# Input x by transposing DMAs in natural row order instead of TensorE transposes, in a fused spectral and state-space kernel

## The chip, the cores and the metric

The kernel runs on one core of a Trainium2 chip. The metric is the device time of one execution in microseconds (us). Five engines run side by side, each with its own queue of instructions that it takes in order: TensorE (PE: matmuls, and the transposes that are written as matmuls), VectorE (DVE), ScalarE (ACT), GpSimd (POOL) and SyncE (SP, which here only issues DMAs). An instruction starts when its engine is free and the data and buffers that it needs are ready.

## The reference

The input x has 2048 tokens of 1024 channels in bf16. Two branches are computed and mixed token by token with a gate:

```python
g = sigmoid((x * gate_w).sum(-1, keepdims=True))
# A: filter in the frequency domain
a = irfft2(rfft2(x) * (w_r + 1j * w_i)).astype(bfloat16)
# B: complex diagonal recurrence with 1024 states
Lam_bar = exp(exp(log_dt) * Lambda)
Bu = x @ (((Lam_bar - 1) / Lambda)[:, None] * Bmat).T
h[t] = Lam_bar * h[t - 1] + Bu[t]
b = 2 * real(h @ Cmat.T) + x * Dskip
out = g * a + (1 - g) * b
```

## The kernel before

**x in two roles.** The tile `xQ` holds x transposed: channels on partitions, in 8 blocks `d8`, and for each of 16 rows j the 128 tokens m*16+j. It is made by `load_x` (L195, eight plain loads of 512 KB into the space of the tiles `CT`, which C fills later) and `turn_x` (L653): eight TensorE transposes into a PSUM tile `pt`, and a copy by ScalarE to `xQ` (L657). That copy also puts the even and the odd m of a row into two halves.

**The front.** `front()` (L768) works through the 16 rows of the spectral branch. Of a row, `fold(j)` (L659) adds and subtracts the two halves of the channels on VectorE into `preT`; `fd(j)` (L332) is the transform along the channels, eight matmuls with the constant `G`, copied out as `X1` (L339); `s1(j)` (L342) is the first step of the transform along the tokens, four matmuls with the constant `T2`, copied out as `A1` (L351) and stored to a scratch in DRAM by SyncE (L353). Before row 8 VectorE does the copy of `A1`, from row 8 on ScalarE. `keep_A1` keeps one column in every 512 of `A1`.

**The tables.** The recurrence is done as a rotation, a real scan, and a rotation back. The rotations need four tables of cosines and sines, made by `make_tab` (L208) for two of eight blocks of states at a time. It is cut into pieces by `yield`, and `front(n)` takes n pieces behind each row. In order, the pieces hold: VectorE's angle and its reduction (L213, L814, L816); ScalarE's Abs and Sin (L818, L819); ScalarE's cosine and scaled sine (L821, L224), with a copy by GpSimd; ScalarE's scaled cosine (L229) with VectorE's first product (L230); VectorE's second product (L235), which shares a piece with the next block's angle. A block of 45 lines of small operations (L825 to L855) runs on VectorE before the tables; it waits for ScalarE's first sines and cosines, and the fold of row 5 is queued behind it.

**The recurrence.** `unit(c, q)` (L253) handles 256 tokens and half of the states, in two halves of 32 matmuls from `xQ` and B into PSUM `psu` (L300), each copied out by ScalarE as `h` (L302). All 16 rows of x enter each of them. Its VectorE work is put into a list `work` as seven pieces with their due costs, 12.7 in all (turn back 2.4, join 1.5, two scans of 2.3, carry 0.4, turn 2.4, join on 1.4), and `vector(us)` takes pieces from that list up to the given amount. `early(tb)` (L579) is the product with C for 128 tokens, also in two halves. `halves(ssm, n)` advances a chain of units and early tiles by n halves. The units 0,0 / 0,1 / 1,0 / 1,1 make up the first eight halves.

**The order by hand.** PE, VectorE and ScalarE run in program order (`manual_schedule`, L169). From row 8 on, each row of the front is followed by one half of the chain, from row 9 with `vector(4.2)`; the matmuls of the gate (L695) stand behind row 10. After the front come seven stages of gfnet, "w", "a", "z", "q", "qn", "s2" and "uv", which correct single columns and start the next transform, with 4, 1, 2, 2, 1, 0 and 1 halves between them and `vector(3.0)` after each half; "w" begins with small matmuls that reverse a vector (L390). Then 16 steps "is1" (L484, L485) follow with one half each, 16 steps "is2", and the output tiles.

**The queues.** SyncE issues the loads of x, G, T2, B, the small constants and C, and the stores of `A1`; B and C are loaded by transposing DMAs (L205, L555). GpSimd issues ten small DMAs of columns of W (`load_Wcols`, L733, behind row 3) and two DMAs of the gate. The order on these two queues is chosen by a scheduler.

**PSUM.** `psA` has two buffers, shared by `fd`, `s1` and the small products; the transposes have two (`psX`), the units one (`psF`) until row 7 and then two (`psU`).

Of the kernel before, what the change touches and what calls it, by code (L numbers as in the profile page):

```python
# [13 lines left out]
FP32 = mybir.dt.float32  # L14
# [14 lines left out]
NHA, NHB = 4, 2  # L29

# [78 lines left out]
def kernel(  # L109
# [55 lines left out]
    xctx = ExitStack()  # L165
    psF = xctx.enter_context(tc.tile_pool(name="psF", bufs=1, space=PSUM, reuse_waits="tile"))
    psX = xctx.enter_context(tc.tile_pool(name="psX", bufs=2, space=PSUM, reuse_waits="tile"))
    pools = {"u": psF}
# [3 lines left out]

    vec8 = tmp.tile([8, 5, P], BF16, name="vec8")
# [13 lines left out]
    xn = [CT[i // 4][:, 2 * (i % 4):2 * (i % 4) + 2, :] for i in range(8)]  # L187
    x_v = x.rearrange("(p j) d -> p j d", j=16)
    fft = {}
    fft["G"] = pre.tile([P, 2, 4, K], BF16, name="G_sb")  # L190
# [3 lines left out]
    def load_x(i):  # L194
        nc.sync.dma_start(out=xn[i], in_=x_v[:, 2 * i:2 * i + 2, :])  # L195
# [55 lines left out]
    x_t = xQ.rearrange("p d j (g q) -> p d g j q", g=2)  # L251

    def unit(c, q):  # L253
# [42 lines left out]
        for ri in range(2):  # L296
            psu = pools["u"].tile([P, 4, TC], FP32, name="psu", tag="psu")
            for j in range(4):
                for d8 in range(8):
                    nc.tensor.matmul(psu[:, j, :], lhsT=BT[4 * q + j][:, ri, d8, :],  # L300
                                     rhs=x_t[:, d8, :, :, 8 * c:8 * (c + 1)], start=(d8 == 0), stop=(d8 == 7))
            nc.scalar.copy(out=u[:, ri].rearrange("p b (q j) -> p b q j", j=32),  # L302
                           in_=psu.rearrange("p b (j q) -> p b q j", j=32))
# [23 lines left out]
    def gfnet():  # L327
# [4 lines left out]
        def fd(j):  # L332
            ps = psA.tile([P, 2, K], FP32, name="ps_fd", tag="ps")
# [5 lines left out]
            (nc.vector.tensor_copy if j in (3,5,7,) else nc.scalar.copy)(out=X1.rearrange("p r (i c) -> p r i c", c=2), in_=ps.rearrange("p c (r i) -> p r i c", r=2))  # L339
            X1s[j] = X1  # L340

        def s1(j):  # L342
# [7 lines left out]
            A1 = CT[0][:, j, :].rearrange("p (g k) -> p g k", g=2) if j < 8 else A1_4[:, j % 4]  # L350
            (nc.vector.tensor_copy if j < 8 else nc.scalar.copy)(out=A1, in_=psa)  # L351
            A1s[j] = A1
            nc.sync.dma_start(out=t1_w[j], in_=A1)  # L353
            if j in (8, 12):
                keep_A1(j - 4)

        def keep_A1(j):
            if j < 8:
# [322 lines left out]
    for i in range(3, 8):  # L681
        load_x(i)
# [287 lines left out]
```

## Time and profile before

| | |
|---|---|
| time, median of 3 runs | 340.88 us (340.6 to 340.92) |
| span of the profiled execution | 338.3 us, from its first to its last instruction |
| busy share of PE, DVE, ACT, POOL | 96%, 86%, 49%, 10% |
| granted TensorE clock | full throughout |
| 128 transposes (L656), busy 0.61 us for eight | within the first 34 us |
| plain loads of x (L195) | 8 of 512 KB, 5.8 us to landing |
| first half of the recurrence, start | 40.46 us |
| first VectorE work of the recurrence, start | 51.81 us |
| last `s1` of the front, start | 81.57 us |
| first "is1" matmul, start | 129.06 us |

The profiled execution's own time is known as its span; the timed runs of the same kernel are 2.6 us above it in the median, which is the work before the first and after the last instruction. Times inside the execution are counted from the start of the span. A matmul is listed with its whole passage through the array, so the next one starts before the listed end: 32 matmuls of a half take 3.67 us, and the next instruction starts 3.5 us after the first.

### The profile page before, as it was taken

What the parts mean: (1) busy time and instruction counts of PE and PEld (TensorE: products, weight loads), DVE (VectorE), ACT (ScalarE), POOL (GpSimd) and SP (SyncE); (2) the same over time, 40 slices, a digit from 0 to 9 for tenths busy, and PEclk for the clock granted to TensorE, in tenths of its full rate; (3) what the DMA queues carried; (4) which work ended last, traced back from release to release, by engine and by line L of the source; (5) the groups of instructions that cost most, each with busy time, mean ns of one, the idle gap of its engine ahead of it and who ended that gap; (6) DMA issues with size and microseconds to landing.
All of it is one profiled execution on the core that took longest, in us unless ns stands there. A gap on an engine that the chain in (4) does not pass through costs nothing.

```text
span 338.3 us, 6201 instructions
## 1 busy us (share of the span) xinstructions
PE 326.3 (96%) x2414; PEld 212.3 (63%) x2446; DVE 292.1 (86%) x449; ACT 167.0 (49%) x211; POOL 32.1 (10%) x64
## 2 busy tenths in 40 slices
PE   8989899999999999999999999999999999999995
PEld 3445465666847575747566575869945876565552
DVE  2679948999999999999999999999980997999951
ACT  3697597836223145656557552646632243443510
POOL 1372012210000000000000000000000011121220
PEclk9999999999999999999999999999999999999999
DMA  7999999998893047889999735947203019856695
GB/s 263 409 192 212 203 217 213 163 215 205 274 213 102 2 129 180 227 202 272 259 284 260 200 135 153 224 127 215 62 2 125 32 31 147 168 109 94 110 145 166
DMA packets 83581, 58.71 MB, mean 174 GB/s; under 512 B 54328, under 2 KB 74304, under 8 KB 83424
## 3 DMA queue, kind: packets, MB, share of 16 engines
q1 hardware_dynamic: 80304, 55.64, 65.5%
q0 software_dynamic: 3168, 2.66, 8.3%
q8 instruction: 19, 0.31, 0.4%
q14 instruction: 10, 0.08, 0.1%
q10 hardware_dynamic: 80, 0.01, 0.0%
HBM read 30.49 MB, written 17.83 MB: 143 GB/s over the span
## 4 chain that ended last, share of the span: by engine, by line
PE 71%; DVE 23%; ACT 2%; issue 2%; DVEq 0%; ACTq 0%
PE ps_y L570 26%; PE psu L300 22%; PE ps_h L570 4%; DVE h L275 4%; PE ps_id L601 4%; PE ps_is L484 2%; PE ps_fd L336 2%; PE ps_is L509 2%; PE ps_is L485 2%; DVE CT L351 2%; PE ps_y L574 2%; PE ps_s L460 2%; DVE h L263 1%; DVE su L262 1%; DVE h L287 1%
## 5 line engine op out<-in xcount | busy, mean ns | idle before, releaser
L300 PE MATMUL psu<-xQ,BT 128*128 128x256 bf16 x1024 | 116.6, 273 | 0.8 <-ACT ye L588 0.5
L300 PEld LDWEIGHTS <-BT 128*128 128x128 bf16 x1024 | 98.8, 98 | 17.5 <-issue 4.5
L570 PE MATMUL ps_y<-CT,h 128*128 128x512 bf16 x436 | 99.5, 379 | 0.6
L570 PEld LDWEIGHTS <-h 128*128 128x128 bf16 x512 | 49.7, 98 | 55.2
L275 DVE TENSOR_TENSOR_SCAN h<-rz,h 128x1024 bf16<-128x1024 f32 x32 | 72.2, 2280 | 0.3
L302 ACT CAST h<-psu 128x1024 bf16<-128x1024 f32 x32 | 32.3, 1011 | 51.4 <-PE psu L300 51.3
L616 POOL DMA_DIRECT2D BT<-y_scratch x10 | 11.9, 1194 | 239.6 <-DVE BT L610 232.0
L588 ACT ACTIVATE ye<-ps_y,omg 128x512 f32<-128x512 f32 x20 | 12.7, 684 | 44.0 <-PE ps_y L574 28.7
L336 PE MATMUL ps_fd<-G_sb,preT 128*128 128x512 bf16 x119 | 29.3, 379 | 2.1 <-ACT X L339 1.0
L262 DVE TENSOR_TENSOR su<-h,tab 128x2048 bf16<-128x2048 bf16 x16 | 19.6, 1223 | 2.8 <-ACT h L302 2.2
L336 PEld LDWEIGHTS <-preT 128*128 128x128 bf16 x128 | 12.0, 97 | 15.4 <-issue 2.8
L287 DVE TENSOR_TENSOR h<-h,tab 128x2048 bf16<-128x2048 bf16 x16 | 20.7, 1295 | 0.5
L462 ACT CAST X<-ps_s 128x1024 bf16<-128x1024 f32 x16 | 16.2, 1014 | 8.7 <-PE ps_s L460 8.7
L263 DVE TENSOR_TENSOR h<-h,tab 128x2048 bf16<-128x2048 bf16 x16 | 19.6, 1225 | 0.8
L286 DVE TENSOR_TENSOR sg<-h,tab 128x2048 bf16<-128x2048 bf16 x16 | 19.5, 1220 | 0.1
L657 ACT COPY xQ<-pt 128x1024 bf16<-128x1024 bf16 x16 | 15.6, 1017 | 2.8 <-PE pt L656 2.7
L511 ACT CAST ZT<-ps_is 128x1024 bf16<-128x1024 f32 x16 | 15.5, 1024 | 2.2 <-PE ps_is L509 2.2
L339 ACT CAST X<-ps_fd 128x1024 bf16<-128x1024 f32 x13 | 13.2, 1012 | 6.2 <-PE ps_fd L336 6.1
L487 ACT CAST C<-ps_is 128x1024 bf16<-128x1024 f32 x16 | 16.1, 1007 | 0.0
L601 PE MATMUL ps_id<-raw,ZT 128*128 128x256 bf16 x128 | 15.9, 273 | 0.0
L570 PE MATMUL ps_h<-CT,h 128*128 128x512 bf16 x62 | 14.4, 379 | 0.1
L601 PEld LDWEIGHTS <-ZT 128*128 128x128 bf16 x128 | 12.4, 98 | 2.2
(186 smaller groups left out, 362.3 us busy)
## 6 DMA issues: line engine op xcount, KB each, us to landing
y_scratch<-ye SPq DMA_DIRECT2D x20, 256.0 KB, 2.6
CT<-in_A_x_dram SPq DMA_DIRECT2D x8, 512.0 KB, 5.8
Bb<-turn_scratch SPq DMA_DIRECT2D x16, 256.0 KB, 4.0
turn_scratch<-C SPq DMA_DIRECT2D x16, 256.0 KB, 3.7
raw<-turn_scratch SPq DMA_DIRECT2D x16, 256.0 KB, 4.2
Wb<-in_A_w_r_dram SPq DMA_DIRECT2D x32, 127.8 KB, 4.2
Wb<-in_A_w_i_dram SPq DMA_DIRECT2D x32, 127.8 KB, 4.1
out_dram<-BT SPq DMA_DIRECT2D x14, 256.0 KB, 2.5
```

What stands on the lines that cost most here:

```text
L262: nc.vector.tensor_mul(out=su, in0=u[:, ::-1], in1=bc(1))
L263: nc.vector.tensor_mul(out=u, in0=u, in1=bc(0))
L275: nc.vector.tensor_tensor_scan(out=seg, data0=rz[:, js].rearrange("p j t -> p (j t)"), data1=seg, initial=0.0, op0=ALU.mult, op1=ALU.add)
L286: nc.vector.tensor_mul(out=sg, in0=u[:, ::-1], in1=bc(3))
L287: nc.vector.tensor_mul(out=u, in0=u, in1=bc(2))
L300: nc.tensor.matmul(psu[:, j, :], lhsT=BT[4 * q + j][:, ri, d8, :], rhs=x_t[:, d8, :, :, 8 * c:8 * (c + 1)], start=(d8 == 0), stop=(d8 == 7))
L302: nc.scalar.copy(out=u[:, ri].rearrange("p b (q j) -> p b q j", j=32), in_=psu.rearrange("p b (j q) -> p b q j", j=32))
L336: nc.tensor.matmul(ps[:, cls, :], lhsT=preTs[j][:, 4 * cls + d4, :], rhs=G_sb[:, cls, d4, :], start=(d4 == 0), stop=(d4 == 3))
L462: nc.scalar.copy(out=X2, in_=ps2)
L487: nc.scalar.copy(out=C1.rearrange("p h (c i) -> p h c i", c=2), in_=psc.rearrange("p h (i c) -> p h c i", c=2))
L570: nc.tensor.matmul(psy, lhsT=hs[c, jb // 4][:, ri, jb % 4, P * tq:P * (tq + 1)], rhs=CT[ri][:, jb, 512 * dh:512 * (dh + 1)], start=(i == 0 ...
L601: nc.tensor.matmul(pse[:, slot, :], lhsT=ZT_t[:, i, tb, :], rhs=fft["Gi"][:, i, :], start=(kb == 0), stop=(kb == 1))
```

## The change

- x is loaded by 16 transposing DMAs on SyncE, one for each row j, straight into `xQ`, with the tokens of a row in natural order. `turn_x`, its copies, and one group of four `keep_warm` matmuls are gone.
- The split into even and odd m moves into `fold`, which now reads `xQ` with a step of two elements. The units and the gate read `xQ` in natural order, and their copies out of PSUM are adapted.
- The order on SyncE is written anew: x and the first eight loads of B interleaved, T2 in between, then the small constants, the other eight of B, and all of C behind the front. G is issued by ScalarE, ahead of the five small vectors.
- Of the `A1` copies, VectorE does rows 6, 8, 10, 12, 14 and 15 and ScalarE the other ten. All sixteen go to `CT` and are stored by GpSimd. ScalarE does all the copies of `X1` (before, VectorE did three).
- `fd` uses the two buffers of `psU`, which the units now have from the start; `psA` is left to `s1` and the small products.
- `front` is the same for all rows: fold two rows ahead, `fd` one row ahead, `s1`, then the table pieces: none to row 3, one for rows 4 to 7, two from row 8. The recurrence joins in from row 14, with one half and `vector(2.0)` behind each of rows 14 and 15. The gate, `keep_A1(1)` and the remaining loads follow the front, then six halves with `vector(3.5)` each, and the stages "w" to "uv" get 7, 1, 1, 1, 1, 0 and 1 halves. `load_Wcols` moves from row 3 to row 12. The chain has unit 2,1 before the first early tile.

```diff
+A1_BY_VECTOR = (6, 8, 10, 12, 14, 15)
...
+    for cls in range(2):
+        nc.scalar.dma_start(out=fft["G"][:, cls], in_=cG[:, cls])
...
-    x_v = x.rearrange("(p j) d -> p j d", j=16)
+    x_v = x.rearrange("(m j) d -> j m d", j=16)
...
-    def load_x(i):
-        nc.sync.dma_start(out=xn[i], in_=x_v[:, 2 * i:2 * i + 2, :])
+    def load_x(j):
+        nc.sync.dma_start_transpose(out=xQ[:, :, j, :], in_=x_v[j])
...
-            ps = psA.tile([P, 2, K], FP32, name="ps_fd", tag="ps")
+            ps = psU.tile([P, 2, K], FP32, name="ps_fd", tag="psu")
...
-            A1 = CT[0][:, j, :].rearrange("p (g k) -> p g k", g=2) if j < 8 else A1_4[:, j % 4]
-            (nc.vector.tensor_copy if j < 8 else nc.scalar.copy)(out=A1, in_=psa)
-            A1s[j] = A1
-            nc.sync.dma_start(out=t1_w[j], in_=A1)
+            A1 = CT[j // 8][:, j % 8, :].rearrange("p (g k) -> p g k", g=2)
+            (nc.vector.tensor_copy if j in A1_BY_VECTOR else nc.scalar.copy)(out=A1, in_=psa)
+            nc.gpsimd.dma_start(out=t1_w[j], in_=A1)
...
-        nc.vector.tensor_add(out=preTs[j][:, 0:4], in0=xQ[:, 0:4, j, :], in1=xQ[:, 4:8, j, :])
-        nc.vector.tensor_sub(out=preTs[j][:, 4:8], in0=xQ[:, 0:4, j, :], in1=xQ[:, 4:8, j, :])
+        to = preTs[j].rearrange("p d (g q) -> p d g q", g=2)
+        lo, hi = (xQ[:, 4 * i:4 * (i + 1), j, :].rearrange("p d (q g) -> p d g q", g=2) for i in range(2))
+        nc.vector.tensor_add(out=to[:, 0:4], in0=lo, in1=hi)
+        nc.vector.tensor_sub(out=to[:, 4:8], in0=lo, in1=hi)
...
+    for j, b in enumerate((0, 0, 0, 0, 0, 1, 0, 1, 0, 1, 0, 1, 1, 1, 1, 1)):
+        load_x(j)
+        if j in (1, 2, 6):
+            load_T2(*{1: (0, 2), 2: (2, 8), 6: (8, 16)}[j])
+        load_B(b)
     assert step() == "front"
-    for j in range(2):
-        turn_x(j)
-        fold(j)
-    keep_warm(4)
+    fold(0)
     fft["fd"](0)
+    fold(1)
...
-        for what in plan.get(j, "fFS"):
...
+        if j + 2 < 16:
+            fold(j + 2)
+        if j + 1 < 16:
+            fft["fd"](j + 1)
+        fft["s1"](j)
...
-        front(0 if j < 4 else 1 if j < 6 else 2 if j < 10 else 3)
-        if j >= 8:
+        front(0 if j < 4 else 1 if j < 8 else 2)
+        if j == 8:
+            fft["keep_A1"](0)
+        if j == 12:
+            load_Wcols()
+        if j >= 14:
             halves(ssm, 1)
-        if j >= 9:
-            vector(4.2)
...
+            vector(2.0)
+    gate()
+    fft["keep_A1"](1)
+    load_small()
+    load_B(8)
...
+    for q in range(8):
         load_C(q)
-    for v, n in (("w", 4), ("a", 1), ("z", 2), ("q", 2), ("qn", 1), ("s2", 0), ("uv", 1)):
+    for _ in range(6):
+        halves(ssm, 1)
+        vector(3.5)
+    for v, n in (("w", 7), ("a", 1), ("z", 1), ("q", 1), ("qn", 1), ("s2", 0), ("uv", 1)):
```

## The prediction

> **What bounds the kernel now.** I read the page first. Its share by engine says that TensorE is nearly full and VectorE not far behind:
>
> ```profile
> span 338.3 us, 6201 instructions
> PE 326.3 (96%) x2414; PEld 212.3 (63%) x2446; DVE 292.1 (86%) x449; ACT 167.0 (49%) x211; POOL 32.1 (10%) x64
> ```
>
> The reader is to see that 12 us of TensorE's span are idle, and that a change is worth what it does to TensorE's queue, or to VectorE's where TensorE waits for it. Next the busy time by stretch, cut at the last row before the recurrence, at the end of the eighth half (85.6), at the first "is1" (129.06) and at the end of that phase; behind the length come PE, PEld, DVE, ACT and POOL:
>
> ```profile
> 7.15:39.92 32.77, 29.34 (x225) 15.22 (x230) 27.84 (x73) 24.81 (x34) 12.83 (x33) 1.00 1.11 265
> 39.92:85.60 45.68, 44.92 (x364) 30.82 (x369) 39.41 (x61) 31.38 (x44) 6.38 (x14) 1.00 1.04 203
> 85.60:129.20 43.60, 42.57 (x350) 29.77 (x352) 41.45 (x75) 13.38 (x17) 0.00 (x0) 1.00 0.56 140
> 129.20:206.60 77.40, 76.98 (x503) 48.45 (x509) 75.84 (x91) 43.58 (x60) 0.00 (x0) 1.00 0.82 221
> ```
>
> From 39.92 on TensorE is full, because each row of the front is followed by a half of the recurrence. From 85.6 VectorE is full too. Last the chain of waits around row 8 (start, us, what), one turn of a loop between VectorE and ScalarE:
>
> ```profile
> 38.99 0.79 DVE tab L235 x2
> 39.77 0.54 DVE ang L213 x2
> ...
> 40.34 0.44 DVE rot_kk L814
> ...
> 40.80 0.70 DVE ang L816
> ...
> 42.58 0.99 ACT X L339
> 43.57 0.91 ACT A L351
> 44.49 0.62 ACT cs_f L821
> 45.11 0.40 ACT t L224
> 45.53 0.92 DVE tab L230 x2
> ...
> 47.12 0.79 DVE tab L235 x2
> ```
>
> From L235 to the next L235 it takes 8.13 us for two rows. VectorE's angle must be done before ScalarE's Abs and Sin; these stand before the copies of `X1` and `A1`, these before the cosine, and VectorE's next product waits for that, with the next fold queued behind it. In the kernel before TensorE has halves of 3.5 us to do meanwhile. That cover is what the change takes away.
>
> **The change part by part.** Prices from the chain and the timeline: eight transposes 0.45 us of TensorE's queue (16 in 0.89), an `fd` 1.74, an `s1` 0.54, a half 3.5 (32 matmuls in 3.49), the gate 1.83 (55.79 to 57.63).
>
> *Transposes, copies, keep_warm.* Before `s1(8)`, 14 groups of transposes go, 6.3 us of TensorE; 16 copies of ScalarE of 1.02 and four `keep_warm` matmuls (1.03, in a gap) go too. ScalarE gets three more `X1` and two more `A1` of 1.01. The second buffer of `psU` for `fd` lets it run one row ahead, so there I let TensorE go at its own pace, 2.28 a row.
>
> *Rows 0 to 8.* The first `fd` stays at 7.15: G landed 6.0 us after an issue at 1.19, and ScalarE issues it only half a microsecond earlier. `s1(8)` has ten `fd`, eight `s1` and a 0.2 us transpose of the vectors ahead: 21.9 us. In between stands the block of small operations, 3.2 us long (21.91 to 25.1). ScalarE's `X1(2)` starts at 13.3 (7.15, three `fd`, one `s1`, 0.2, 0.2 of passage); behind it come `A1(1)`, Abs 0.2, a table load 1.28, Sin 0.2, `X1(3)` and `A1(2)`: with copies at 0.91 each the cosine runs at 18.6, the block at 18.9 to 22.1, and `fd(5)` at 22.9, where TensorE was free at 18.4. So `s1(8)` starts at 7.15 + 21.9 + 4.5 + 0.2 = 33.8, against 39.92: 6.1 us gained here.
>
> *Rows 8 to 14.* The turn of 8.13 stays, as the pieces come at two per row. It gets longer by `A1` of the even row, now on VectorE between the fold and L235 (1.14), and by the fold's step of two. No row has a bf16 operation with such a step; the ends are 0.42 (the contiguous L661, same size) and 0.69 (L816, the same size in f32), so 0 or 0.54 per turn. I take the upper end: what is read lies 4 bytes apart, as in the f32 row. Turn: 8.13 + 1.14 + 0.54 = 9.8.
>
> [...]
>
> The first L235 comes at 33.8 + 0.65 + 1.15 = 35.6 (behind `A1(8)`), the next at 45.4 and 55.2. Behind the third are the angle and its reduction (2.4), so `fold(15)` runs at 57.6, `fd(15)` at 58.3, `s1(14)` at 60.0. TensorE needed 6 x 2.28 = 13.7 of these 26 us. The two halves behind rows 14 and 15 end at 60.6 + 3.5 + 0.54 + 3.5 = 68.1; gate and six halves: 90.9. The eighth half, gate included, ended at 85.6 before. TensorE is 5.3 late.
>
> *The recurrence on VectorE.* Its first piece needs the second half's copy: 68.1 + 1.2 = 69.3, against 51.81. Up to the first product with W, `vector` is given 2 + 6 x 3.5 + 11 x 3.5 = 61.5: four units of 12.5 (0,1 took 72.59 to 85.02) and 11.1 of the fifth. The small blocks of the stages add 7.4 (sums of their durations between 91.3 and 123.2), and waits 2.1 (43.6 less 41.45 in the third stretch). So 70.6, then 1.7 for the products: "is1" starts at 141.6. TensorE's own work from 90.9 (six halves of 3.5, six of 3.67, 3.2 small) would end at 137.1, so VectorE decides. By then the chain has one half more than before; less 3.5 that is 138.1 against 129.06: 9.0 late. In the "is1" phase a step takes 4.84 of TensorE (134.03 to 201.73 in 14) and 3.3 + 1.4 of VectorE; TensorE was full there and stays so, and nothing is made up.
>
> *A1 stored by GpSimd.* SyncE is rid of 16 issues of 0.53, and ScalarE of its two waits for an `A1` buffer (5.7 us, for which TensorE waited 0.3). GpSimd gets 16 issues of about 1.19 (L616). Ten small DMA issues of GpSimd ran from 18.6 to 26.2 while VectorE worked, and one held it:
>
> ```profile
> 22.60 0.82 DVE L842 TENSOR_SCALAR nr<-lbr 128x8 f32<-128x8 f32 x1
> ```
>
> Its sister L837 took 0.17, and it ended at 23.42 with GpSimd's L738. Ends: 0 and 16 x 0.65 = 10.4. A gain is excluded, as nothing else waited for SyncE's issues. I take one hold in ten, 16 x 0.065 = 1.0.
>
> [...]
>
> *x by DMA.* A transposing DMA took 1.28 to 1.31 us of SyncE when the queue moved, and 2.65 when plain loads were ahead (three in 7.96). Row 15 is behind 22 others (16 x, 7 B in all) and three loads of 0.4: it lands at about 36 at best, 66 at worst. The nearest stretch, 13 in 21.9 us with four stores between, gives 1.69 each, so 44. `fold(15)` needs it at 57.6: hidden, as is every earlier row. Its rows are 32 KB apart in DRAM, as in the plain loads, which ran at over 400 GB/s.
>
> *Moved and hidden.* C comes after the last `A1` store (about 73, by 5.5 to landing), eight of its sixteen transposes before that; at 1.69 each the rest is there at about 90, and the first early tile needs it at 105. The columns of W move from row 3 to row 12: ten issues and 7.6 us of GpSimd, with stores and table copies behind them; used at 91. The gate's two DMAs land by 86, used at 101. The other eight B land by 57, used at 70. Natural order in the units costs nothing that a row shows. The clock was halved at the start (eight `keep_warm` matmuls 3.60, four later ones 1.03); half speed in rows 8 to 14 would need 4.6 of the 4.9 us per row, so the loop covers it. After the gap of 4.5 before `fd(5)` a drop would cost up to 9 in rows 5 to 8; no row shows one behind a gap (the clock is full in all four stretches), and I take 0.
>
> **Sum.** 338.3 + 9.0 + 1.0 = 348.3 us of span. The timed median stands 2.6 above the span, so 351.
>
> **The rivals.**
> - *Faster: the loop of the tables does not pace the front.* Then rows 8 to 14 go at 2.28, the halves end at 55.5, VectorE starts at 56.7, "is1" at 129.0 with one half more: 3.6 gained, 337. For it speak the six extra microseconds at row 8 and the 10 us of removed work; against it the measured turn of 8.13, all of whose members are left. It decides if a turn is under 6.8 (three turns, 9.0).
> - *x arrives late.* At 2.65 each, `fold(15)` waits till 66: 8.4 more, 359. It decides from about 2.3 each; against it, 1.69 beside stores.
> - *GpSimd's stores hold VectorE.* Ten stores lie in the looped rows; at 0.65 each 6.5 instead of 1.0, 356.
>
> **How the numbers follow.** A kernel of this kind tells 0.2% from no change. Forecast as reasoned, 347.5 to 354.5: 0.62. Late x 0.10. Held VectorE 0.16. The fast front 0.09, a front between that comes out even 0.03. So faster 0.09, same 0.02, slower 0.89. The range leaves out the fast cases and the worst of late x: 345 to 360.
>
> **What would show it.** In the profile after: `s1(8)` near 34; L235 about 9.8 apart from row 8; TensorE half idle from 34 to 60, with waits of `fd` for `preT` of 2 to 3 us; the first half near 60.6; turn back near 69; "is1" near 141.6; TensorE full afterwards. The fold at 0.69 shows the step. I am wrong if the pieces run ahead of the rows, if `fold` waits for DMAs, or if VectorE's small operations swell beside GpSimd's issues.

## The result, and the profile after

The changed kernel takes 363.36 us (median of four runs, 360.53 to 363.56), the kernel before 340.9 beside it: 1.0623 times as long, with a 95% interval of 1.0573 to 1.0674. The forecast was 351, in a range of 345 to 360. The sign was right and more than half of the loss was missing: 22.5 us instead of 10. All times below are medians without three runs (one of e6, two of e15) that lay over 1.5% above the fastest of their kernel.

The profiled execution has a span of 361.7 us (its own run took 363.51). Here is the summary of the page after:

```profile
span 361.7 us, 5961 instructions
PE 328.7 (91%) x2314; PEld 205.1 (57%) x2314; DVE 295.2 (82%) x443; ACT 156.8 (43%) x200; POOL 45.8 (13%) x80
```

TensorE (PE) has 132 weight loads (PEld) fewer, those of the 128 transposes and the four `keep_warm` matmuls, and is still busy for 2.4 us more: some of its matmuls ran at half speed (from 57.99 to 61.50 the granted clock was 0.50, and an `fd` took 3.60 us instead of 1.90). Its idle time went from 12 to 33 us. The next fence is the busy time by stretch, cut where it was cut before; behind the length stand PE, PEld, DVE, ACT and POOL, then the granted clock:

```profile
7.15:39.92 32.77, 25.02 (x112) 8.36 (x113) 20.56 (x58) 19.42 (x27) 11.61 (x26) 0.84 1.10 205
39.92:85.60 45.68, 30.11 (x167) 13.01 (x169) 25.81 (x46) 23.26 (x37) 18.70 (x31) 0.81 1.12 217
85.60:129.20 43.60, 43.60 (x398) 35.49 (x387) 41.91 (x54) 12.52 (x14) 2.60 (x8) 1.00 0.71 133
129.20:206.60 77.40, 75.61 (x533) 47.78 (x532) 75.47 (x106) 38.11 (x55) 0.00 (x0) 1.00 0.70 190
```

Up to 85.6 neither TensorE nor VectorE is full, and the clock stands at 0.84 and 0.81, where it was 1.00 before. From there on TensorE is full and VectorE nearly so (43.60 and 41.91 of 43.60). So the loss arises ahead of 86 us. VectorE's first piece of the recurrence starts at 86.0 instead of 51.8; the way from there to "is1" is then 7.4 us shorter than before, as no tables and folds stand between its pieces, and from "is1" on nothing is made up: it starts at 155.9 and the span ends 205.8 us later. Before, that last stretch took 209.2 us and held one half of the recurrence (3.5) more, which is the same.

How the start looks, in the timelines of VectorE and TensorE (start, us, engine, line, work; in brackets the idle time before and what ended it):

```profile
10.21 0.69 DVE L649 TENSOR_TENSOR preT<-xQ 128x512 bf16<-128x512 bf16 x1 [9.04 <-DMA xQ<-in_A_x_dram]
```

```profile
10.96 3.59 PE L334 MATMUL ps_fd<-G_sb,preT 128*128 128x512 bf16 x8 [6.17 <-DMA vec<-in_B_Lambda_im_dram]
14.96 0.17 PE L752 MATMUL vps<-ident,vec 8*128 8x8 bf16 x1 [0.21 <-DMA vec<-in_gate_w_dram]
15.07 1.90 PE L334 MATMUL ps_fd<-G_sb,preT 128*128 128x512 bf16 x8
```

The first row of x lands at 10.2, the last of the five vectors at 15. The first `fd` starts at 10.96, not at 7.15. The profile names a vector's load for its wait, but what it reads is the first half of `fold(0)`, which ended at 10.90. It takes 3.59 us where 1.90 is usual, and the second stands behind the transposes of the vectors. `s1(8)` starts at 41.30 (forecast 33.8).

The chain of waits at the first turn of the loop of the tables (L234 is the L235 of before):

```profile
44.70 5.59 DMA Wp<-in_A_w_i_dram
...
51.90 0.55 POOL tab L219
...
53.02 0.99 ACT X L337
54.01 0.92 ACT CT L349
54.92 0.62 ACT cs_f L781
55.55 0.40 ACT t L223
55.97 1.37 DVE tab L229 x2
...
59.67 0.79 DVE tab L234 x2
```

Before, this chain held VectorE and ScalarE alone. Now GpSimd is in it: a load of W's columns, and the cast of the table behind it. From L234 to L234 it takes 16.5 us at the first turn, then 10.24 and 9.04 (forecast: 9.8 each). GpSimd's and ScalarE's timelines say why:

```profile
36.51 0.23 POOL L710 COPY Wp<-xQ 128x64 bf16<-128x64 bf16 x1 [10.66 <-DMA xQ<-in_A_x_dram]
49.53 0.26 POOL L723 COPY Wc<-Wp 128x30 bf16<-128x30 bf16 x1 [2.78 <-DMA Wp<-in_A_w_i_dram]
51.83 0.62 POOL L219 CAST tab<-sn_f 128x512 bf16<-128x512 f32 x1
```

```profile
52.48 0.63 ACT L779 ACTIVATE sn_f<-ang 128x512 f32<-128x512 f32 x1 [6.15 <-POOL tab L219]
```

The columns of W begin with a copy out of row 12 of x, so they can't start before that row lands (36.51). Ten loads follow and three copies that wait for their landing, with two stores of `A1` among them (45.37 and 50.98). The cast of the table, behind all that on GpSimd's queue, runs at 51.83. ScalarE's Sin for the next table waits for it, since it writes over what the cast reads; `X1` stands behind the Sin, and `s1` waits for `X1`.

### The profile page after: what moved, and what is told of

Its sections match the earlier page's. It is cut to its first block, busy times and chain, and to the rows that moved or that the text cites. A ratio compares the mean times of both kernels' runs of the same rounds, so it can differ in the third digit from the quotient of the medians.

```text
span 361.7 us, 5961 instructions
## 1 busy us (share of the span) xinstructions
PE 328.7 (91%) x2314; PEld 205.1 (57%) x2314; DVE 295.2 (82%) x443; ACT 156.8 (43%) x200; POOL 45.8 (13%) x80
## 4 chain that ended last, share of the span: by engine, by line
PE 60%; DVE 21%; SPq 8%; DMA 5%; ACT 2%; issue 2%; POOL 1%; DVEq 0%; ACTq 0%; POOLq 0%
PE ps_y L562 22%; PE psu L298 19%; DVE h L273 6%; SPq L194 6%; PE ps_h L562 4%; PE ps_id L593 3%; SPq L204 2%; PE ps_is L501 2%; PE ps_is L476 2%; PE ps_is L477 2%; DMA Wp<-in_A_w_r_dram 2%; PE ps_s L452 2%; DVE su L260 2%; DVE h L261 2%; DMA Wp<-in_A_w_i_dram 2%
## 5 line engine op out<-in xcount | busy, mean ns | idle before, releaser
L298 PE MATMUL psu<-xQ,BT 128*128 128x256 bf16 x1024 | 115.2, 273 | 0.8 <-ACT ye L580 0.5
L562 PE MATMUL ps_y<-CT,h 128*128 128x512 bf16 x448 | 101.3, 379 | 0.0
L334 PE MATMUL ps_fd<-G_sb,preT 128*128 128x512 bf16 x128 | 37.4, 445 | 19.7 <-DVE preT L649 13.5
L454 ACT CAST X<-ps_s 128x1024 bf16<-128x1024 f32 x16 | 16.2, 1014 | 10.9 <-PE ps_s L452 10.9
L261 DVE TENSOR_TENSOR h<-h,tab 128x2048 bf16<-128x2048 bf16 x16 | 19.6, 1225 | 0.8
L285 DVE TENSOR_TENSOR h<-h,tab 128x2048 bf16<-128x2048 bf16 x16 | 19.6, 1225 | 0.5
L337 ACT CAST X<-ps_fd 128x1024 bf16<-128x1024 f32 x16 | 16.1, 1006 | 8.1 <-PE ps_fd L334 8.1
L649 DVE TENSOR_TENSOR preT<-xQ 128x512 bf16<-128x512 bf16 x16 | 11.1, 695 | 9.0 <-DMA xQ<-in_A_x_dram 9.0
L229 DVE SCALAR_TENSOR_TENSOR tab<-cs_f,cr,t 128x256 bf16<-128x256 f32 x8 | 4.8, 642 | 14.7 <-ACT t L223 14.7
L346 PE MATMUL ps_s<-X,raw 64*128 64x512 bf16 x64 | 11.1, 428 | 5.7 <-ACT X L337 5.7
```

The costliest lines, as they stand in the source:

```text
L261: nc.vector.tensor_mul(out=u, in0=u, in1=bc(0))
L285: nc.vector.tensor_mul(out=u, in0=u, in1=bc(2))
L334: nc.tensor.matmul(ps[:, cls, :], lhsT=preTs[j][:, 4 * cls + d4, :], rhs=G_sb[:, cls, d4, :], start=(d4 == 0), stop=(d4 == 3))
L454: nc.scalar.copy(out=X2, in_=ps2)
L562: nc.tensor.matmul(psy, lhsT=hs[c, jb // 4][:, ri, jb % 4, P * tq:P * (tq + 1)], rhs=CT[ri][:, jb, 512 * dh:512 * (dh + 1)], start=(i == 0 ...
```

## The experiments

One table holds what was read from the profiles of the kernels that keep the changed kernel's order of work. "Turn" is the distance between the first two L234 (or the line that answers to it), "half" the first half of the recurrence, "turn back" VectorE's first piece, all in us; the time is the median of the runs.

| kernel | fold(0) | first fd | s1(8) | turn | half | turn back | is1 | end after is1 | time |
|---|---|---|---|---|---|---|---|---|---|
| forecast | | 7.15 | 33.8 | 9.8 | 60.6 | 69.3 | 141.6 | | 351 |
| changed | 10.21 | 10.96 | 41.30 | 16.5 | 77.1 | 86.0 | 155.9 | 205.8 | 363.36 |
| e1 W columns early | 10.41 | 11.16 | 51.99 | 10.24 | 81.6 | 90.6 | 160.4 | 205.6 | 364.99 |
| e4 G behind row 0 | 4.46 | 8.50 | 39.05 | 13.97 | 72.5 | 81.4 | 151.3 | 206.1 | 358.65 |
| e5 W columns late | 11.48 | 12.22 | 43.33 | 10.23 | 72.9 | 81.9 | 151.7 | 205.6 | 358.36 |
| e6 A1 by SyncE | 11.71 | 12.46 | 43.18 | 11.19 | 71.6 | 80.5 | 150.4 | 205.6 | 356.85 |
| e7 e4 + keep_warm | 4.40 | 8.48 | 36.19 | 18.01 | 73.2 | 82.4 | 152.2 | 205.6 | 359.45 |
| e13 e4 + e5 | 4.47 | 8.74 | 38.90 | 10.23 | 68.4 | 77.3 | 147.2 | 206.6 | 353.93 |
| e9 e4 + e5 + keep_warm | 4.47 | 7.49 | 35.20 | 10.24 | 63.1 | 72.1 | 142.0 | 205.6 | 349.86 |

Two columns make the reading easy. From "is1" on every one of these kernels needs 205.6 to 206.6 us. And from turn back to "is1" each needs 69.8 or 69.9. So the whole difference is made before VectorE's first piece of the recurrence. One column is a warning: with G on ScalarE's queue `fold(0)` starts anywhere from 8.75 to 11.71 in executions whose loads of x and G are programmed alike, so a single profile's "is1" carries up to 3 us that no edit made.

**e1: the columns of W early.** Back behind row 3, and filled with zeros first, so that no row of x is waited for.

```diff
-        nc.gpsimd.tensor_copy(out=Wp.rearrange("p r b c -> p (r b c)"), in_=xQ[:, 0, 12, 0:64])
-        nc.gpsimd.tensor_copy(out=Wf, in_=xQ[:, 0, 12, 0:2])
+        nc.gpsimd.memset(Wp, 0.0)
+        nc.gpsimd.memset(Wf, 0.0)
...
-        if j == 12:
+        if j == 3:
```

> The columns of W are loaded behind row 3 again, and Wp and Wf are filled with zeros instead of being copied from row 12 of x; all else is as in the changed kernel. Theory (GpSimd's ten loads and their copies hold the table casts): in the changed kernel the cast L219 ran only at 51.83 and the turn between the first two L234 took 16.5 us; here that turn is 9 to 10.5 us, the first half starts near 70 instead of 77, and the time falls by 5 to 7 us, to 356 to 358. Rival (the long turn has another cause, a late row of x or the clock, and the casts were no more than the last to arrive): the turn stays over 14 us and the time within 1.5 us of 363.4.

Measured 364.99: no gain at all, though the turn is 10.24 as the theory has it. TensorE's timeline shows where it went:

```profile
20.96 0.42 PE L752 MATMUL vps<-ident,vec 8*128 8x8 bf16 x2 [4.47 <-DMA vec<-in_B_log_dt_dram]
22.04 0.18 PE L752 MATMUL vps<-ident,vec 8*128 8x8 bf16 x1 [0.66 <-DMA vec<-in_gate_w_dram]
22.15 3.59 PE L334 MATMUL ps_fd<-G_sb,preT 128*128 128x512 bf16 x8
```

The loads of the columns went out from 1.97 on, although the program has them behind row 3: with nothing left to wait for, the scheduler of GpSimd's queue put them first. Beside them the vectors landed at 22 instead of 15 and a row of x was late as well (a wait of 5.91 at VectorE's second fold); the second `fd` began 7 us later than in the changed kernel and `s1(8)` 10.7 later. The experiment changed two things at once; e5 takes its place.

**e2: the halves back in the front.** Seven halves behind rows 9 to 15, one after the front, VectorE's pieces from row 11, the last eight B behind all of x.

```diff
-        if j >= 14:
-            halves(ssm, 1)
-            vector(2.0)
+        if j in (6, 7):
+            load_B(4)
+        if j >= 9:
+            halves(ssm, 1)
+        if j >= 11:
+            vector(3.5)
...
-    for _ in range(6):
-        halves(ssm, 1)
-        vector(3.5)
+    halves(ssm, 1)
+    vector(7.0)
```

> Seven of the eight first halves of the recurrence stand behind rows 9 to 15 again, one after the front, VectorE's pieces behind rows 11 to 15, and the last eight transposes of B are issued behind all of x; the amounts are those of the changed kernel. Theory (the moved halves are the larger part of the loss: the loop's waiting time lies empty on both engines): VectorE was busy for only 25.8 of the 45.7 us after 39.92; it can start the recurrence near 60 instead of 86, some 12 us of its pieces fit into waiting time, and the time falls by 8 to 13 us, to 350 to 355. Rival (what is put into the front makes the loop's turns longer by as much): 360 or more, with the distance between two L234 at 14 us or more in each turn.

Measured 358.45, between the two. The recurrence starts on VectorE at 66.98 instead of 86.02, but the turns became 16.2, 14.9 and 13.9, and "is1" comes at 149.6, 6.2 earlier. Some 1.1 of that is an earlier start in this execution (`s1(8)` at 40.17 instead of 41.30). The lost cover is real, and most of what it would give back is taken by a longer loop, as the rival has it; the columns of W still stand in the first turn.

**e3: one table piece per row.**

```diff
-        front(0 if j < 4 else 1 if j < 8 else 2)
+        front(0 if j < 4 else 1)
```

> From row 8 on each row issues one piece of the tables instead of two, so that one turn of the loop between VectorE and ScalarE covers four rows; the rest of the tables comes after the gate, ahead of the second unit. Theory (the loop of the tables paces rows 8 to 14): the front ends some 14 us earlier (the last s1 near 66 instead of 80.66), two turns of tables remain behind it (about 8 us of VectorE, of which TensorE's halves hide most), and the time falls by 5 to 10 us, to 353 to 358. Rival (the rows are paced by something else: x, the clock, the stores): s1(15) stays after 76 and the time within 2 us of 363.4.

Measured 359.82, 3.5 less where the theory had 5 to 10. The last `s1` starts at 68.55 instead of 80.66 and the first half at 64.95, 12 us earlier: the loop does pace the rows, and the rival falls. But "is1" comes only 3.0 earlier. The two turns that are left run after the front (L234 at 76.47 and 82.09), on an engine that has the recurrence to do by then; the second unit's turn back moved from 98.56 only to 94.02.

**e4: G behind the first row of x.**

```diff
-    for cls in range(2):
-        nc.scalar.dma_start(out=fft["G"][:, cls], in_=cG[:, cls])
...
         load_x(j)
+        if j == 0:
+            for cls in range(2):
+                nc.sync.dma_start(out=fft["G"][:, cls], in_=cG[:, cls])
```

> G is loaded on SyncE's queue, behind the first transposing load of x, as in the kernel before, and not on ScalarE's; the vectors come first on ScalarE's queue. Theory (the first row of x lands late, at about 10.2, since it runs beside 1 MB of G): row 0 lands by 5, the first fd starts at 7 to 8.5 instead of 10.96, s1(8) comes 2 to 4 us earlier than 41.3, and the time falls by 2 to 4 us, to 359 to 361. Rival (the first transposing DMA is slow by itself, 9 us from issue to landing): the first fd starts at 10 to 13 (G now comes behind it), and the time is 363 to 366.

Measured 358.65. `fold(0)` starts at 4.46, and in every kernel with G in this place it does so at 4.40 to 4.51; in the six with G on ScalarE's queue it starts at 8.75 to 11.71. The transposing load of row 0 (256 KB), issued at 0.74, was in use 3.7 us later here; in the changed kernel, with the 1 MB of G beside it from another queue, it took 9.4 us from issue to landing, and all that reads it waits.

What that is worth can't be read from e4 alone. `s1(8)` starts 2.25 us earlier, but the columns of W do not (36.83 instead of 36.51). The turn ends 4.8 earlier because the scheduler of GpSimd's queue happened to put the table cast at 47.52, ahead of the last two loads of the columns and of their copies, so that ScalarE's Sin waited 3.37 us instead of 6.15. The pair that differs in G's place alone, without the columns in the way, is e5 and e13: there `s1(8)` comes 4.4 and "is1" 4.5 us earlier.

**e5: the columns of W late.** They are filled from the tables that the last cast writes, and so come behind it.

```diff
-        nc.gpsimd.tensor_copy(out=Wp.rearrange("p r b c -> p (r b c)"), in_=xQ[:, 0, 12, 0:64])
-        nc.gpsimd.tensor_copy(out=Wf, in_=xQ[:, 0, 12, 0:2])
+        nc.gpsimd.tensor_copy(out=Wp.rearrange("p r b c -> p (r b c)"), in_=tab[:, 0, 7, 0:64])
+        nc.gpsimd.tensor_copy(out=Wf, in_=tab[:, 0, 7, 0:2])
...
-        if j == 12:
-            load_Wcols()
...
     tctx.close()
+    load_Wcols()
```

> The columns of W are loaded behind the last table cast on GpSimd's queue (Wp and Wf are first filled from the tables that this cast writes, and no longer from row 12 of x). e1 mended the long turn (16.5 to 10.2 us between L234s) and lost it again, as its ten small loads ran beside the first rows of x and held them (fd(1) at 22.15 instead of 15.07); here they run late. Theory (the columns of W held the casts): the first turn is 9.5 to 10.5 us, the first half starts at 70 to 71.5 instead of 77.06, and the time falls by 5 to 7 us, to 356 to 358. Rival (the first turn is long for another reason): it stays over 14 us and the time within 1.5 us of 363.4.

Measured 358.36. VectorE's timeline at the first turn:

```profile
45.14 0.86 DVE L234 SCALAR_TENSOR_TENSOR tab<-sn_f,cr,t 128x256 bf16<-128x256 f32 x2
55.37 0.87 DVE L234 SCALAR_TENSOR_TENSOR tab<-sn_f,cr,t 128x256 bf16<-128x256 f32 x2
```

10.23 instead of 16.5. The 6.3 us at the turn became 4.2 at "is1", as this execution was 2.0 late at `s1(8)`: its first row of x came at 11.48.

**e6: A1 stored by SyncE.**

```diff
-            nc.gpsimd.dma_start(out=t1_w[j], in_=A1)
+            nc.sync.dma_start(out=t1_w[j], in_=A1)
```

> A1 is stored by SyncE again, all else as in the changed kernel. Theory (the stores of GpSimd hold nothing that counts; the forecast had 1.0 us for them): the stores now stand behind the loads of x on SyncE's queue and start after 43 us, nobody waits for them before C is loaded, and the time changes by -1.5 to +1.5 us. Rival (GpSimd's stores hold VectorE): VectorE's pieces get shorter and the time falls by 4 us or more.

Measured 356.85, the size that the rival gave, by another way. The first turn fell to 11.19. Without the stores among the loads of W's columns the table cast ran at 48.85 instead of 51.83, and as this execution was 1.9 later at `s1(8)`, ScalarE's Sin waited 1.27 for it instead of 6.15. VectorE itself was hardly held: the other two turns are 0.44 shorter each. e14 separates the two.

**e7: e4 with a warm clock.** Eight more `keep_warm` matmuls at the start, twelve in the gap ahead of `fd(5)`.

```diff
-    keep_warm(8)
+    keep_warm(16)
...
         fft["s1"](j)
+        if j == 3:
+            keep_warm(12)
```

> As e4, and eight more keep_warm matmuls at the start, and twelve behind s1(3), in the gap in which TensorE waits for the fold before fd(5). In e4 fd(0) took 3.57 us, fd(1) 2.53 and fd(5) 2.60 with the next s1 and fd slow as well, where 1.90 is the usual. Theory (the clock falls after a gap of some 4 us, and the rows up to 8 are TensorE's pace): fd(0) and fd(5) take 1.9 to 2.2 us, s1(8) starts 2 to 4 us before the 39.05 of e4, and the time is 1.5 to 4 us under e4's 358.65. Rival (the slow matmuls lie beside other waits, or the clock does not follow the gaps): s1(8) within 1 us of e4, the time within 1 us of it.

Both at once: `fd(5)` takes 1.90 us instead of 2.60, `fd(0)` 2.34, a short wait for G included, instead of 3.57, and from the same first `fd` (8.48, 8.50) `s1(8)` starts 2.9 us before e4's, as the theory has it; the time is 359.45, 0.8 above e4's, as the rival has it. The timelines of GpSimd, ScalarE and VectorE show what took it:

```profile
35.64 0.98 POOL L711 COPY Wp<-xQ 128x64 bf16<-128x64 bf16 x1 [11.24 <-DMA xQ<-in_A_x_dram]
37.98 0.87 DVE L232 SCALAR_TENSOR_TENSOR tab<-sn_f,cr,t 128x256 bf16<-128x256 f32 x2
47.55 0.63 ACT L782 ACTIVATE sn_f<-ang 128x512 f32<-128x512 f32 x1 [6.32 <-POOL tab L217]
55.99 0.86 DVE L232 SCALAR_TENSOR_TENSOR tab<-sn_f,cr,t 128x256 bf16<-128x256 f32 x2
```

The columns of W hang on the landing of row 12, which no faster front brings forward. So the turn ends at 55.99, where e4's ended at 54.81, and grows to 18.0. As long as they stand there, what is gained ahead of 38 us need not count, and the order that the scheduler chose on GpSimd's queue decides.

**e9: all three.** e4, e5 and e7's `keep_warm` in one kernel, the order of work kept.

> The changed kernel with the three things that the forecast left out taken away at once, and its order of work kept: G behind the first row of x (e4), the columns of W behind the last table cast (e5), the keep_warm matmuls of e7. Theory (the three are the whole of the miss): s1(8) at 36 to 37 as in e7, L234 to L234 10.2 us from the first turn on, the first half near 64 to 66, is1 at 142.5 to 145, and the time is 349 to 353, the forecast being 351. Rival (something else is missing, and takes up what these give, as the columns of W did in e7): the time stays over 355.

Measured 349.86 (1.0277 times the kernel before, 1.0212 to 1.0342). The profile's VectorE timeline:

```profile
37.01 0.87 DVE L232 SCALAR_TENSOR_TENSOR tab<-sn_f,cr,t 128x256 bf16<-128x256 f32 x2
47.25 0.86 DVE L232 SCALAR_TENSOR_TENSOR tab<-sn_f,cr,t 128x256 bf16<-128x256 f32 x2
57.48 0.86 DVE L232 SCALAR_TENSOR_TENSOR tab<-sn_f,cr,t 128x256 bf16<-128x256 f32 x2
66.51 0.86 DVE L232 SCALAR_TENSOR_TENSOR tab<-sn_f,cr,t 128x256 bf16<-128x256 f32 x2
```

Turns of 10.24, 10.23 and 9.03, "is1" at 142.0. With the three things that the forecast left out taken away, "is1" and the time come out where it put them, and 9.5 us over the kernel before remain. The agreement to 0.4 us at "is1" is partly luck: VectorE's first piece of the recurrence starts 2.8 us later than forecast, and the way from there to "is1" is 2.4 shorter.

**e13: e9 without the additional keep_warm.**

> e9 without the twenty additional keep_warm matmuls: G behind the first row of x, the columns of W behind the last table cast, nothing else. Theory (the cold clock is a term of its own, 2 to 3 us): fd(0), fd(5) and their neighbours are slow as in e4, s1(8) starts at 37.5 to 39.5 instead of 35.20, is1 comes 2 to 3.5 us after the 142.0 of e9, and the time is 351.5 to 353.5. Rival (the slow matmuls lie beside other waits): is1 and time within 1 us of e9 (349.86).

Measured 353.93, 4.1 above e9, somewhat more than the theory had; beside the kernel before, which was measured with each, it is 1.0341 against 1.0277, which is 2.2. "is1" is 5.3 later in the profiled executions. TensorE's timeline:

```profile
8.74 3.57 PE L332 MATMUL ps_fd<-G_sb,preT 128*128 128x512 bf16 x8 [3.93 <-DMA G_sb<-c_G]
26.00 2.98 PE L332 MATMUL ps_fd<-G_sb,preT 128*128 128x512 bf16 x8 [3.73 <-DVE preT L647]
54.25 3.43 PE L332 MATMUL ps_fd<-G_sb,preT 128*128 128x512 bf16 x8 [1.49 <-DVE preT L647]
64.48 3.43 PE L332 MATMUL ps_fd<-G_sb,preT 128*128 128x512 bf16 x8 [2.46 <-DVE preT L647]
```

Behind gaps of 3.9, 3.7, 1.5 and 2.5 us an `fd` takes 3.57, 2.98, 3.43 and 3.43 where 1.90 is usual. Of the 5.3 us, 1.25 are no matter of the clock: G landed that much later in this execution than in e9's (first `fd` at 8.74 and 7.49). The slow matmuls up to `s1(8)` make 2.5, near the 2.9 of e7 against e4, and the slow last `fd` 1.5. That last one has no additional matmul near it, and of the kernels that have them all e10 shows it too (3.60 at 59.26, behind a gap of 0.92) and e9 does not (1.90 at 60.78, behind 1.10); what decides it no run shows. The clock is a term of the sum, of 2.5 to 4 us.

**e14: e9 with A1 stored by SyncE.** The edit of e6.

> e9 with A1 stored by SyncE. Theory (without the columns of W ahead of the casts the stores cost only the 0.4 us per turn by which the cast L223 slips beside VectorE's product, 1.28 instead of 0.91 us in e6): turns of 9.8 and 8.6 instead of 10.24 and 9.03, is1 1 to 1.5 us earlier, the time 348 to 349.5. Rival (the stores hold more than that, as the 6 us of e6 would have it): the time under 346.

Measured 350.51: nothing gained. The turns are 9.80, 9.80 and 8.60, as expected, 0.43 shorter each. VectorE's product behind the cosine, in its timeline, first in e9 and then in e14:

```profile
43.70 1.28 DVE L227 SCALAR_TENSOR_TENSOR tab<-cs_f,cr,t 128x256 bf16<-128x256 f32 x2 [2.76 <-ACT t L221]
```

```profile
44.77 0.92 DVE L227 SCALAR_TENSOR_TENSOR tab<-cs_f,cr,t 128x256 bf16<-128x256 f32 x2 [2.76 <-ACT t L221]
```

In e9 a store (42.95, 0.73) stands ahead of the cast on GpSimd's queue, so that the cast starts at 43.68, with the product; in e14 it has started 0.37 before the product and is half done. What the three turns gave (1.3) went into a start that was 1.1 later (G landed later, `s1(8)` at 36.33), and both kernels have their first half at 63. With the columns of W out of the way the stores cost about 1 us in the turns; the 6 us of e6 belong to the columns.

**e10: the fold without its step of two.** As e9; the fold writes in the order in which it reads, and the reordering of the rows is left out, so that the GFNet part is computed from mixed-up rows.

```diff
-        nc.vector.tensor_add(out=to[:, 0:4], in0=lo, in1=hi)
-        nc.vector.tensor_sub(out=to[:, 4:8], in0=lo, in1=hi)
+        nc.vector.tensor_add(out=preTs[j][:, 0:4], in0=xQ[:, 0:4, j, :], in1=xQ[:, 4:8, j, :])
+        nc.vector.tensor_sub(out=preTs[j][:, 4:8], in0=xQ[:, 0:4, j, :], in1=xQ[:, 4:8, j, :])
```

> As e9, with the fold writing its rows in the order in which it reads them, without the step of two; the reordering is left out, so that the rows of the GFNet part are mixed up. Theory (the strided fold is a term of the loop): a fold's two halves take 0.42 us each and no longer 0.69, a turn is 0.5 us shorter with its one or two folds on VectorE's chain, four turns and the folds before them give 2 to 4 us, and the time falls under e9 by that. Rival (the folds lie in VectorE's waiting time): no turn shorter by more than 0.2 us, and the time within 1 us of e9.

Measured 348.66, 1.2 under e9, with intervals that overlap; "is1" is at 142.2, 0.2 later than e9's. The fold's halves take 0.42 and the first two turns 9.71 and 9.70, so 0.53 of each turn is the fold's step, as the forecast took it. At "is1" it bought nothing, since two other limits are near. VectorE's timeline:

```profile
29.23 0.42 DVE L645 TENSOR_TENSOR preT<-xQ 128x512 bf16<-128x512 bf16 x1 [2.17 <-DMA xQ<-in_A_x_dram]
34.70 0.43 DVE L645 TENSOR_TENSOR preT<-xQ 128x512 bf16<-128x512 bf16 x1 [0.73 <-DMA xQ<-in_A_x_dram]
```

The rows of x come no sooner than the faster folds ask for them; and the last `fd`, at 59.26, fell into the slow clock (3.60 us).

**e8, e11, e12, e15: towards a version that is not slower.** e8 takes e9's three edits and moves work: all of B behind all of x, one table piece in rows 4 to 11 and two from row 12, halves behind rows 12 to 15 and four after the gate.

```diff
+        if j == 8:
+            load_B(8)
+        if j >= 12:
+            halves(ssm, 1)
         if j >= 14:
-            halves(ssm, 1)
-            vector(2.0)
+            vector(2.5)
...
-    for _ in range(6):
+    for _ in range(4):
         halves(ssm, 1)
-        vector(3.5)
+        vector(4.5)
```

> G behind the first row of x on SyncE, the columns of W behind the last table cast, the keep_warm matmuls of e7; all sixteen transposes of B issued behind all of x; one table piece in rows 4 to 11 and two from row 12; four halves of the recurrence behind rows 12 to 15 and four after the gate, with VectorE's pieces from row 14. Theory (start, W columns, clock and lost cover are the whole of the loss, and TensorE has 7 us less to do than before): x has landed near 33, the front ends before 66, the first half starts at 46 to 52, is1 at 129 to 138, and the time is 337 to 347. Rival (VectorE's longer folds and the order of its pieces keep it late): is1 after 142 and the time over 351.

Measured 345.81 (1.0132, 1.0108 to 1.0157): first half 47.54, "is1" 138.3. In TensorE's timeline the late columns of W show up as a new wait:

```profile
87.87 0.16 PE L380 MATMUL Wrev_ps<-Wc,JP_sb 128*128 128x4 bf16 x1 [4.72 <-POOL Wc L725]
```

e11 lays their loads behind the second cast, lets ScalarE copy them, stores A1 by SyncE, and issues two rows of the front (two more calls of `front`) ahead of VectorE's block of small operations:

> e8 with four edits. The copies of the columns of W are ScalarE's and come behind the gate, their loads behind the second table cast, since in e8 TensorE waited 4.7 us for them at the first product with Wc; A1 is stored by SyncE; two more rows of the front are issued ahead of VectorE's block of small operations, where it waits for the cosine (in e8 TensorE had 4.3 us without a row there, filled by keep_warm, which falls away); and pieces of the tables begin one row later. Theory (these waits are on the path): the first half starts at 43 to 46 instead of 47.54, is1 at 130 to 134, and the time is 336 to 342, level with the kernel before or up to 1.5% faster. Rival (VectorE is full and takes the gain, or B is not there): is1 after 136, the time over 343.

Measured 342.42 (1.0057, 1.0026 to 1.0089), "is1" at 134.4: between the two, with a new wait once more, this time at the first early tile:

```profile
100.90 5.42 PE L560 MATMUL ps_y<-CT,h 128*128 128x512 bf16 x15 [5.23 <-DVE omg L692]
```

The profile names `omg`; what was late is more likely C, whose second eight transposes SyncE issued from 92.02 on, behind the last store of A1 (84.30), which reads what they overwrite. e12 gives the stores of rows 8 to 15 back to GpSimd, and `vector` 3.0 instead of 3.5 us ahead of "is1" and 2.4 instead of 2.0 in the is2 phase:

> e11 with two edits. The A1 of rows 8 to 15 are stored by GpSimd again: on SyncE's queue the last of them went out at 84.30, behind eight transposes of C, and the other eight, which overwrite what it reads, began only at 92.02, so that TensorE stood for 5.23 us before 100.90 at the first early tile. And VectorE's pieces are given 3.0 instead of 3.5 us in each of the twelve steps ahead of is1, and 2.4 instead of 2.0 in the is2 phase, as VectorE is full from 61 on and would not let TensorE use what it gains. Theory (C and VectorE's allotment are what is left ahead of is1): no wait over 2 us at the first early tile, is1 at 127 to 131, and the time is 335.5 to 339.5, faster than the kernel before by 0.3 to 1.5%. Rival (VectorE's pieces are due anyway, and the deferred ones hold TensorE later): is1 is early, but TensorE waits in the phases behind it, and the time is 341 to 344.

Measured 340.49 (0.9989, 0.9960 to 1.0017): level with the kernel before, and a little short of the theory. "is1" comes at 132.2, the wait at the early tile is gone, and the deferred pieces hold nobody: the end is 205.6 behind "is1", as ever. TensorE was busy for 321.9 us, 4.4 less than before. The wait that is next in its timeline is for B:

```profile
60.00 1.05 PE L296 MATMUL psu<-xQ,BT 128*128 128x256 bf16 x8 [1.09 <-DMA BT<-in_B_B_re_dram]
```

e15 lets GpSimd store all of A1, so that B comes sooner, and puts the half's copy ahead of the table pieces in rows 12 to 15:

> e12 with two edits. All A1 are stored by GpSimd, so that the eight stores on SyncE's queue (5.45 us) no longer stand ahead of the last eight transposes of B, for which TensorE waited 2.7 us in the third half; and in rows 12 to 15 the half's copy by ScalarE stands ahead of the row's two table pieces, since TensorE waited 2.55 us for a PSUM buffer whose copy stood behind an Abs that waited for VectorE. Theory (TensorE is the limit from 65 to is1 in e12, these waits set it back): is1 at 127 to 130.5 instead of 132.2, the time 336 to 339, faster than the kernel before by 0.5 to 1.5%. Rival (other waits of the same size take their place, VectorE's ahead of all): is1 after 131.5, the time 339.5 to 342.

Measured 340.32, with a ratio of 0.9954, 0.9916 to 0.9993: half a per cent under the kernel before, barely clear of level, and where the rival put it. Its profile, of an execution that took 343.37, has "is1" at 135.8 and still 3.7 us of waits for B, so the theory is not borne out; what its fastest runs (337.35) did better stays open.

## Why the prediction missed: its steps

**Right.** The loop of the tables between VectorE and ScalarE paces rows 8 to 14 once the halves no longer lie between them: e3, which loosens it, brings the last `s1` 12 us forward. Its turn was forecast at 9.8 and is 10.24, 10.23 and 9.03 in e9, and 9.80, 9.80 and 8.60 in e14, without GpSimd's stores. The fold's step of two costs 0.69 instead of 0.42 per half and 0.53 per turn (e10), the end that was taken, though "is1" did not gain by the shorter fold. TensorE full behind "is1" and nothing made up there: in every kernel. The moved cover as the reason for the sign: e2 gets some 5 us of it back at "is1", and e8, which differs from e9 in where the halves, the pieces and B stand, is 4.1 us faster than e9. That is less than half of the 9.5 us that e9 is above the kernel before; the way on to e12, which is level, took other edits as well, so how much of the 9.5 is cover stays open.

**Failed: "The first `fd` stays at 7.15".** That step looked at G and not at what G does to the others. G was one of two things that the first `fd` needs; the other, row 0 of x, now ran beside G and landed 9.4 us after its issue, and of the vectors, now behind G on ScalarE's queue, the last landed at 15. `fold(0)` started at 10.21, and the first `fd` 3.8 us late. With G behind row 0 `fold(0)` starts at 4.46 (e4), and "is1" comes 4.5 us earlier (e13 against e5). The first `fd` then waits for G and starts at 7.43 to 8.74; no kernel reached 7.15.

**Failed: the columns of W, costed at nothing.** The forecast counted ten issues and 7.6 us on GpSimd, noted that table casts stood behind them, and took their own use at 91 us as the only deadline. Left out were the landing that the copies wait for, the row of x that the first copy waits for, and who waits for the casts: ScalarE's Sin, 6.15 us, with `X1` and `s1` behind it. The kernel before had the landing in its timeline of GpSimd, the first and the last copy of the columns there:

```profile
18.07 0.24 POOL L730 COPY Wp<-CT 128x64 bf16<-128x64 bf16 x1 [3.92 <-DMA CT<-in_A_x_dram]
29.65 0.18 POOL L746 COPY Wc<-Wf 128x2 bf16<-128x2 bf16 x1
```

From the start of the one to the end of the other it is 11.8 us; the 7.6 are the issues alone. The cost is 6.3 us in the first turn, and 4.2 at "is1" (e5, whose start was 2.0 later). Once it is there it can also hide a gain ahead of it (e7).

**Failed: the clock, "I take 0".** The forecast said that no row shows a drop behind a gap. In the profile of before no named wait of TensorE is longer than 1.2 us, so it has no gap like the 4.5 in question to show one behind; the bound, up to 9, was right to stand and wrong to drop. Here `fd` takes up to 3.60 us, at a granted clock of 0.50, and the cost is 2.5 to 2.9 us at `s1(8)` (e13 against e9, e7 against e4). The loop covers half speed in its rows, as the forecast said (e14's turns are the 9.8 of the forecast with `fd` of 2.5 to 3.4 in them), but not in the last `fd`, which comes behind it and took 3.46 in the changed kernel. What sets the drop off no run shows: slow rows stand behind gaps of 3.9, 3.7, 2.5 and 1.5 us (e13) and of 0.9 (e10), and `fd` took its usual 1.90 behind one of 2.2 (e13, at 44.09).

**Mis-sized.** GpSimd's stores: the 1.0 us is about what e9 and e14 differ by in their turns (1.3), and the 10.4 us of the forecast's upper end are excluded by e14. The way was another: of VectorE's operations in the turn, L210 beside an issue (e9, 47.62) took 0.66 us instead of the 0.60 of e14, and the product beside the cast, which slips behind a store, 1.28 instead of 0.92. The stretch from turn back to "is1" is 69.9 us, not 72.3, in every kernel that keeps the order of work. VectorE decides it, as forecast; in e9 its four units and the fifth's pieces run from 72.10 to 140.01, 67.9 us, of which 61.1 are the pieces as priced. So the small blocks and the waits are 6.8 and not 9.5, and the products behind them take 1.95 and not 1.7. The other way, turn back is 2.8 late even in e9: 1.4 at `s1(8)` (35.20 instead of 33.8), 0.9 in two turns and the rest behind them. The late x is no rival for the folds: after row 0 none in the changed kernel waited for a row, though the columns of W waited for row 12. But the margin is thin, as e10 shows.

**The sum again.** In the profiled executions "is1" came 14.3 us after the forecast's 141.6. Taking away G, the columns and the cold clock moves it by 13.9, to 142.0. One edit after the other, from the changed kernel to e5, e13 and e9, the columns give 4.2, G 4.5 and the additional matmuls 5.3, of which 1.25 are G's chance landing. In another order they would divide otherwise: with the columns still there the matmuls gave nothing (e7 against e4). What is left, 0.4, is the 2.8 and the 2.4 above, which nearly cancel.

The rivals named fared no better: none gave these three, and the worst of them ended at 359.

## What to carry to other kernels

When an engine's work is moved in time, look at what stands behind it in order on the same queue and at who waits for that; a late deadline of the moved work itself says nothing. When cover is taken away from TensorE, expect gaps; here the granted clock was 0.50 behind one of 2.90 us, an `fd` took 3.60 us there instead of 1.90, and twenty idle matmuls at the start and in one gap bought 2.5 to 2.9 us. A gain ahead of a wait that hangs on a load's landing can be worth nothing until that wait is gone, so experiments on causes in a row have to be combined before one of them is judged; and where a scheduler orders a queue, look whether an edit changed that order too.

## What the runs showed of the hardware

- A transposing load of 128 rows (256 KB) was in use 4.4 to 4.5 us after the start when it ran ahead of the 1 MB of G, and 8.75 to 11.71 when it ran beside it; with eight loads of W's columns, a few KB each in small pieces, beside them from 2 us on, the vectors landed 7 us later still (e1).
- Where TensorE was half idle, the eight matmuls of an `fd` took up to 3.6 us instead of 1.90, and the length of the gap just ahead did not decide alone: 3.43 behind 1.49 us (e13, at 54.25) and 3.60 behind 0.92 (e10, at 59.26), but 1.90 behind 2.72 (e3, at 62.58).
- Two of VectorE's products (L227, both operands in f32) took 0.92 us when GpSimd's cast of 0.61 was half done at their start, and 1.28 when it began with them (e14, e9).
